# Keys and queries loaded as six adjacent tokens a partition instead of two, put in order by ScalarE's copies

## The chip, the cores and the metric

The kernel runs on one core of a Trainium2 chip. The metric is the device time of one execution in microseconds; lower is better. Engines are named as the profile names them: PE is TensorE's matmul, PEld its weight load, DVE is VectorE, ACT is ScalarE, POOL is GpSimd, SP is SyncE, whose queue issues most of the DMAs.

## What is computed

Four batches of attention with 8 heads, 768 tokens and 64 channels a head, followed by a Fourier mixing block with a two-layer network. All is fp32; the two weight matrices arrive as float64.

```
k_sum = max of k over blocks of 32 tokens      # 24 block keys a head
v_sum = mean of v over the same blocks
s_l   = q k^T / 8, only where |i - j| < 16
s_s   = q k_sum^T / 8 + log(32)
a     = softmax over [s_l, s_s];   attn = a [v, v_sum]
x     = attn as (batch, 768, 512)
u     = x + Re(FFT over tokens and channels of x)
un    = normalize(u) per token
out   = u + relu(un @ w_ch1) @ w_ch2           # 512 -> 2048 -> 512
```

## The kernel before

Heads are handled in pairs: batch b has pairs g = 0 to 3, and a pair's 2 x 64 channels fill the 128 partitions. For the scores, keys and queries must lie with channels on partitions and tokens along the row: `kt` (keys, with a margin of 16 zero columns at each end) and `qt` (queries). In HBM they lie the other way, token by token, so they are transposed on the chip.

**Loading.** `load(b, g)` fetches k, then q, of a pair into a tile `nat` of shape [128, 2, 3, 128] (four buffers; the profile calls its two uses `kn` and `qn`). Up to pair (2, 0), that is for 9 pairs and 18 DMAs of 384 KB, the layout is for TensorE: partition p of head e holds, for each of three groups j, the tokens 256j + 2p and 256j + 2p + 1. Two adjacent tokens are a run of 512 bytes in HBM. Later pairs are loaded in another layout and transposed by DVE; the change leaves them alone. Every load goes through `fetch` (L553) on SP's queue, for which the order of the program is kept in the first part of the kernel.

**Transposing.** `prepare(b, g)` makes kt and then qt.

- In batch 0 (`is_wide`), a matmul with the identity (L702) takes 64 channels of one head, one j and one parity s of the token, and writes 128 columns of a PSUM bank at every second place, so that the bank holds the tokens in order. Groups j = 0, 1 fill a bank of 512 columns, group 2 one of 256. A ScalarE copy (L704) brings each to SBUF, both sides consecutive.
- In batch 1 and pair (2, 0), a transpose (L710) turns both tokens at once, so that the parity s ends up in PSUM's partition half; two ScalarE copies (L712) of [64, 384] a head write to every second column of the destination: 8 copies a pair.

After that DVE takes the maximum over blocks of 32 keys (`km`, L717).

**Order.** `first_attention` lays out batch 0 by hand for PE and DVE: pair (0, 0)'s scores, the next pair's transposes, its scores, the values of the pair before, and so on. In `wide_scores` the scores are made in two halves of 384 tokens: matmuls of L733 (windows of 96 keys against 64 queries) and L737 (block keys), then an exponential on ACT (L739) and a product on DVE. `sum_values` brings block values to SBUF (L752, on ACT or DVE), and `wide_values` (L760) multiplies by the values `vw`, which are loaded in runs of 256 bytes. Then, in SP's order, come the Fourier tables `fs` and `fd` and the first weights (`words`), and the loads of batch 1's pairs.

Behind that, several generators run interleaved: the Fourier part of batch 0 (`y` L1193 with copies L1198, `mx` L1220, normalization L1264 on ACT and L1267 on DVE, transposes `unt` L1271), the conversion of float64 weights (L1052 to L1062 on DVE, L1054 and L1055 on ACT), the attention of batch 1 (scores L776, block scores L792, exponentials L782 and L793, values L809 and L814), and the network's first layer (`hx`, `hy`, `hz` L1293 with ACT copies L1304, L1309, L1311) and second (`o` L1335). Where a bank of L1293 is copied out by L1309 and then accumulated further, the later matmul waits for the copy.

Of the kernel before, what the change touches and what calls it, by code (L numbers as in the profile page):

```python
# [16 lines left out]
P = 128  # L17
# [473 lines left out]
def _main_program(ctx, tc, q, k, v, moe_w_ch1, moe_w_ch2, out):  # L491


    nc = tc.nc
    B, H, S, D = q.shape
    DM = H * D
    DF = moe_w_ch1.shape[1]
    NST = S // P
# [27 lines left out]
    ident = cpool.tile([P, P], FP, name="ident")  # L526
# [24 lines left out]
    def fetch(out, in_):  # L551

        ins = nc.sync.dma_start(out=out, in_=in_)  # L553
        if in_order[0]:
            tc.keep_in_program_order(ins)

    def abank(shape, name):
        return psum.tile(shape, FP, tag="attn", bufs=4, name=name)

    def bank(shape, name):  # L560
        return psum.tile(shape, FP, tag="bank", bufs=4, name=name)
# [12 lines left out]
    def load(b, g, *which):  # L574

        for n in which or (1, 0):
            t = nat[b, g, n] = apool.tile([P, 2, NST // 2, 2 * D], FP, tag="nat", bufs=4, name=f"{'qk'[n]}n_{b}_{g}")
            if (b, g) > (2, 0):
                t = nat[b, g, n] = t.rearrange("p e j n -> p (e j n)").rearrange("p (m c) -> p m c", c=32)
                for e in range(2):  # L580
                    for h in range(2):
                        r, o = D * e + 32 * h, (q, k)[n][b, 2 * g + e].offset + 32 * h
                        fetch(out=t[r:r + 32], in_=bass.AP((q, k)[n].tensor, o, [[D, 32], [32 * D, S // 32], [1, 32]]))
                continue
            fetch(out=t.rearrange("p e j n -> p (e j) n"),
                  in_=(q, k)[n][b, 2 * g:2 * g + 2].rearrange("e (j p s) d -> p (e j) (s d)", p=P, s=2))

# [95 lines left out]
    def prepare(b, g, *which):  # L685
        qn, kn = (nat[b, g, n] for n in range(2))
        kt, km = kt_bufs[g % 2], km_bufs[g % 2]
        qt = apool.tile([P, S], FP, tag="qt", name=f"qt_{b}_{g}") if 0 in (which or (0,)) else None
        for n in which or (1, 0):
            src, dst = (kn, kt[:, W:W + S]) if n else (qn, qt)  # L690
            if (b, g) > (2, 0):
                with tc.issue_after(marks["dense"]):
                    nc.vector.transpose(out=dst, in_=src.rearrange("p m c -> p (m c)"))
                continue
            if is_wide(b):
                for j0, j1 in ((0, 2), (2, 3)):
                    n = 2 * P * (j1 - j0)
                    ps = bank([P, n], f"qk_{b}_{g}_{j0}")
                    for j in range(j0, j1):
                        for s in range(2):  # L700
                            for e in range(2):
                                nc.tensor.matmul(ps[D * e:D * (e + 1), 2 * P * (j - j0) + s:2 * P * (j - j0 + 1):2],  # L702
                                                 src[:, e, j, D * s:D * (s + 1)], ident, start=True, stop=True)
                    nc.scalar.copy(out=dst[:, 2 * P * j0:2 * P * j1], in_=ps)  # L704
            else:
                for e in range(2):

                    ps = abank([P, S2], f"qk_{b}_{g}_{e}")
                    for j in range(NST // 2):
                        nc.tensor.transpose(ps[:, P * j:P * (j + 1)], src[:, e, j, :], ident)  # L710
                    for s in range(2):
                        nc.scalar.copy(out=dst[D * e:D * (e + 1), s:S:2], in_=ps[D * s:D * (s + 1)])  # L712
        if which == (0,):
            nat[b, g] = qt
            return
        with tc.issue_after(marks["fold", 0]) if (b, g) == (1, 0) else ExitStack():
            nc.vector.tensor_reduce(out=km[:, 0:nb], in_=kt[:, W:W + S].rearrange("p (n f) -> p n f", f=BLOCK),  # L717
                                    op=ALU.max, axis=AX.X)
        nat[b, g] = qt
# [110 lines left out]
    def first_attention():  # L830
# [3 lines left out]
        wt["fold"] = split_fold(0, fold)  # L834
        p = {0: wide_scores(0, 0, lambda: add_blocks(0))}
        prepare(0, 1)
        sum_values(0, 0)
        load(0, 3)
        for g in range(NP - 1):
            p[g + 1] = wide_scores(0, g + 1, (lambda: add_blocks(1)) if g == 1 else None)  # L840
            wide_values(0, g, p[g], x)
            load_values(*following(0, g, 2))
            for par in range(2):
                fold_sequence(par, g)
            if g == 0:
                get_tables(0)
            if g < NP - 2:
                prepare(0, g + 2)
                sum_values(0, g + 1)
            if g == NP - 3:  # L850
                load_raw(1)
                load(1, 0)
                load_raw(2)
                sum_values(0, g + 2)
# [105 lines left out]
    def gen_attention(b):  # L960
# [3 lines left out]
        if b == 2:  # L964
            load(2, 1)
            load(2, 2)
        for g in range(NP + 1):
# [36 lines left out]
            if n1:  # L1004
                prepare(*n1, *((1,) if b > 1 else ()))
# [388 lines left out]
    ps = bank([P, 512], "warm")  # L1394
# [19 lines left out]
    for vw in vw_bufs:  # L1414
        nc.gpsimd.tensor_copy(out=vw[:, :, D].rearrange("p (e n) -> p e n", e=2),
                              in_=count[:, None, :].to_broadcast([P, 2, NQ]))
# [47 lines left out]
    for b in range(B):  # L1464
# [14 lines left out]
        if b == B - 2:  # L1479
# [9 lines left out]
            ps = bank([1, 1], "flag_ps")  # L1489
# [42 lines left out]
```

## Time and profile before

| | us |
|---|---|
| median of 3 runs (807.29 to 811.65) | 810.48 |
| profiled execution | 811.17 |
| its span, first to last instruction | 809.3 |
| PE busy | 781.9 (97%) |
| PE weight loads busy | 571.9 (71%) |
| DVE busy | 500.8 (62%) |
| ACT busy | 224.3 (28%) |
| POOL busy | 46.8 (6%) |

Busy time is the union of an engine's instructions. The profile divides the span into 40 slices; the DMA engines are nine tenths busy or more in most of the first slices and less later. SP's hardware queue (q1) moved 133,920 packets and 118.53 MB. The 18 loads concerned are listed as `kn<-in_k_dram` x9 and `qn<-in_q_dram` x9, 384 KB each, with 5.4 and 7.8 us from issue to landing in the median. L712 appears with 40 copies of [64, 384], L704 with 8 of [128, 512] and 8 of [128, 256].

### The profile page before, as it was taken

What the parts mean: (1) busy time and instruction counts of PE and PEld (TensorE: products, weight loads), DVE (VectorE), ACT (ScalarE), POOL (GpSimd) and SP (SyncE); (2) the same over time, 40 slices, a digit from 0 to 9 for tenths busy, and PEclk for the clock granted to TensorE, in tenths of its full rate; (3) what the DMA queues carried; (4) which work ended last, traced back from release to release, by engine and by line L of the source; (5) the groups of instructions that cost most, each with busy time, mean ns of one, the idle gap of its engine ahead of it and who ended that gap; (6) DMA issues with size and microseconds to landing.
All of it is one profiled execution on the core that took longest, in us unless ns stands there. A gap on an engine that the chain in (4) does not pass through costs nothing.

```text
span 809.3 us, 14447 instructions
## 1 busy us (share of the span) xinstructions
PE 781.9 (97%) x5914; PEld 571.9 (71%) x5914; DVE 500.8 (62%) x1135; ACT 224.3 (28%) x493; POOL 46.8 (6%) x85
## 2 busy tenths in 40 slices
PE   8959899999999989999999999999999999999997
PEld 6758665555579856678669876688669875786686
DVE  5778998887998664554476734554476722532352
ACT  3523865543635112200126112200126102001200
POOL 0010000000000220010030300000030000000000
PEclk9979999999999999999999999999999999999999
DMA  9999799769655367939344248511514043205001
GB/s 218 222 198 179 162 320 271 155 224 298 214 165 174 93 202 184 206 86 173 117 176 153 66 160 174 156 48 53 227 40 153 37 171 149 87 0 228 0 28 55
DMA packets 135258, 121.83 MB, mean 151 GB/s; under 512 B 94448, under 2 KB 116688, under 8 KB 134992
## 3 DMA queue, kind: packets, MB, share of 16 engines
q1 hardware_dynamic: 133920, 118.53, 53.3%
q0 software_dynamic: 576, 2.10, 0.8%
q8 instruction: 48, 0.79, 0.4%
q10 hardware_dynamic: 688, 0.20, 0.1%
q14 instruction: 26, 0.21, 0.1%
HBM read 97.22 MB, written 23.59 MB: 149 GB/s over the span
## 4 chain that ended last, share of the span: by engine, by line
PE 89%; DVE 5%; ACT 2%; DMA 2%; SPq 1%; issue 1%; POOL 0%; DVEq 0%; ACTq 0%; POOLq 0%
PE hx L1293 20%; PE ox L1358 17%; PE hz L1293 10%; PE oz L1358 9%; PE o L1335 5%; PE hy L1293 5%; PE oy L1358 4%; PE y L1193 3%; PE sc L776 2%; PE mx L1152 2%; PE av L814 1%; PE av L809 1%; PE unt L1271 1%; DVE w L566 1%; SPq L553 1%; PE qk L702 1%
## 5 line engine op out<-in xcount | busy, mean ns | idle before, releaser
L1293 PE MATMUL hx<-u,w 128*128 128x384 f32 x512 | 187.2, 493 | 3.8 <-DVE h L566 3.8
L1293 PEld LDWEIGHTS hx<-u,w 128*128 128x128 f32 x512 | 95.7, 191 | 72.3 <-DVE h L566 5.7
L1293 PE MATMUL hz<-u,w 128*128 128x384 f32 x256 | 93.2, 487 | 0.0
L1358 PE MATMUL oz<-w,s 128*128 128x256 f32 x336 | 81.6, 380 | 0.6 <-DVE w L566 0.6
L1358 PE MATMUL ox<-w,s 128*128 128x256 f32 x336 | 80.3, 380 | 1.3 <-DVE x L566 1.3
L1358 PE MATMUL ox<-w,h 128*128 128x256 f32 x336 | 79.6, 380 | 0.0
L566 DVE TENSOR_TENSOR x<-ox,x 128x256 f32<-128x256 f32 x84 | 35.3, 422 | 69.5 <-PE ox L1358 69.2
L1293 PEld LDWEIGHTS hz<-u,w 128*128 128x128 f32 x256 | 48.5, 190 | 34.0 <-ACT h L1311 0.5
L1358 PEld LDWEIGHTS oz<-w,s 128*128 128x128 f32 x336 | 63.3, 190 | 10.6 <-issue 1.2
L1358 PEld LDWEIGHTS ox<-w,s 128*128 128x128 f32 x336 | 63.1, 190 | 10.7 <-DVE x L566 2.3
L1358 PEld LDWEIGHTS ox<-w,h 128*128 128x128 f32 x336 | 63.2, 190 | 9.6 <-DVE x L566 0.3
L1304 ACT COPY h<-hx 128x384 f32<-128x384 f32 x32 | 15.3, 479 | 169.9 <-PE hx L1293 169.9
L1293 PE MATMUL hy<-u,w 128*128 128x384 f32 x128 | 46.7, 488 | 0.0
L566 DVE TENSOR_TENSOR h<-hx,h 128x384 f32<-128x384 f32 x32 | 17.8, 555 | 46.4 <-PE hx L1293 46.1
L566 DVE TENSOR_TENSOR h<-hy,h 128x384 f32<-128x384 f32 x32 | 17.8, 555 | 45.3 <-PE hy L1293 45.3
L1320 ACT ACTIVATE h<-hx 128x384 f32<-128x384 f32 x32 | 15.7, 491 | 94.5 <-PE hx L1293 94.5
L1335 PE MATMUL o<-w,h 128*128 128x512 f32 x96 | 41.8, 593 | 0.0
L1358 PE MATMUL oy<-w,h 128*128 128x256 f32 x168 | 40.2, 379 | 0.0
L1293 PEld LDWEIGHTS hy<-u,w 128*128 128x128 f32 x128 | 24.1, 190 | 16.3
L566 DVE TENSOR_TENSOR x<-oz,x 128x256 f32<-128x256 f32 x42 | 17.7, 422 | 28.8 <-PE oz L1358 28.5
L1358 PEld LDWEIGHTS oy<-w,h 128*128 128x128 f32 x168 | 31.9, 190 | 4.3
L1335 PEld LDWEIGHTS o<-w,h 128*128 128x128 f32 x96 | 18.1, 190 | 21.9 <-issue 20.6
(164 smaller groups left out, 1099.5 us busy)
## 6 DMA issues: line engine op xcount, KB each, us to landing
w<-dw SPq DMA_DIRECT2D x44, 896.0 KB, 5.6
words<-in_moe_w_ch_dram SPq DMA_DIRECT2D x32, 512.0 KB, 6.6
dw<-w SPq DMA_DIRECT2D x12, 896.0 KB, 6.2
vw<-in_v_dram SPq DMA_DIRECT2D x47, 192.0 KB, 5.2
out_dram<-x SPq DMA_DIRECT2D x24, 256.0 KB, 2.2
vb<-in_v_dram SPq DMA_DIRECT2D x24, 192.0 KB, 4.0
kn<-in_k_dram SPq DMA_DIRECT2D x9, 384.0 KB, 5.4
qn<-in_q_dram SPq DMA_DIRECT2D x9, 384.0 KB, 7.8
```

The costliest lines, as they stand in the source:

```text
L553: ins = nc.sync.dma_start(out=out, in_=in_)
L566: return nc.vector.tensor_tensor(out=out, in0=in0, in1=in1, op=op).ins
L702: nc.tensor.matmul(ps[D * e:D * (e + 1), 2 * P * (j - j0) + s:2 * P * (j - j0 + 1):2], src[:, e, j, D * s:D * (s + 1)], ident, start=True, ...
L776: nc.tensor.matmul(ps[h][r:r + 64, i, :], kt[rows, o:o + 64], qt[rows, o:o + BLOCK], start=True, stop=True)
L809: nc.tensor.matmul(av[r][32 * j:32 * (j + 1), t, :], p[rows, h, i - NB2 * h, :], vw[rows, i, :], start=(t == 0), stop=False, skip_group_ch ...
L1152: nc.tensor.matmul(out, y[:, g], table, start=False, stop=True, skip_group_check=True)
L1193: nc.tensor.matmul(y, fgs[b][par][:, st, P * g:P * (g + 1)], fs[par][:, g % 2, st, :], start=(st == 0), stop=(st == n - 1))
L1293: ins = nc.tensor.matmul(ps, w[:, a, kk, :], u[:, r, kk, :], start=start and kk == 0, stop=stop and kk == 1, skip_group_check=True)
L1304: nc.scalar.copy(out=c11, in_=X)
L1320: nc.scalar.activation(out=c21, in_=X, func=AF.Relu)
L1335: nc.tensor.matmul(ps, h[:, n, hf, P * t:P * (t + 1)], wt[2, b, j][:, 2 * hf:2 * hf + 2, :], start=(n, hf) == (0, 0), stop=(n, hf) == (NC ...
L1358: nc.tensor.matmul(ps, left[a][:, n, :], wt[2, b, j][:, r, :], start=start and n == 0, stop=stop and n == NC - 1, skip_group_check=True)
```

## The change

Partition p now holds the six adjacent tokens 6p to 6p + 5 of a head, so that a run in HBM is 6 x 256 = 1536 bytes. The number of DMAs and their bytes stay. In batch 0 the matmuls write 128 consecutive columns for each of the six places c = 2j + s within a partition, and the copy puts them in order by writing with a step of six elements (24 bytes). In the later pairs the transposes stay as they are, and each copy's destination has a step of six elements within a group j, and of two between groups, where it had a step of two.

```diff
-            fetch(out=t.rearrange("p e j n -> p (e j) n"),
-                  in_=(q, k)[n][b, 2 * g:2 * g + 2].rearrange("e (j p s) d -> p (e j) (s d)", p=P, s=2))
+            fetch(out=t.rearrange("p e j n -> p e (j n)"),
+                  in_=(q, k)[n][b, 2 * g:2 * g + 2].rearrange("e (p j s) d -> p e (j s d)", p=P, s=2))
...
                             for e in range(2):
-                                nc.tensor.matmul(ps[D * e:D * (e + 1), 2 * P * (j - j0) + s:2 * P * (j - j0 + 1):2],
-                                                 src[:, e, j, D * s:D * (s + 1)], ident, start=True, stop=True)
-                    nc.scalar.copy(out=dst[:, 2 * P * j0:2 * P * j1], in_=ps)
+                                c = P * (2 * (j - j0) + s)
+                                nc.tensor.matmul(ps[D * e:D * (e + 1), c:c + P], src[:, e, j, D * s:D * (s + 1)], ident,
+                                                 start=True, stop=True)
+                    nc.scalar.copy(out=dst.rearrange("r (p c) -> r c p", c=NST)[:, 2 * j0:2 * j1],
+                                   in_=ps.rearrange("r (c p) -> r c p", p=P))
...
                     for s in range(2):
-                        nc.scalar.copy(out=dst[D * e:D * (e + 1), s:S:2], in_=ps[D * s:D * (s + 1)])
+                        nc.scalar.copy(out=dst[D * e:D * (e + 1)].rearrange("r (p j s) -> r s j p", j=NST // 2, s=2)[:, s],
+                                       in_=ps[D * s:D * (s + 1)].rearrange("r (j p) -> r j p", p=P))
```

## The prediction

> **What bounds the kernel now.** I began with busy time by stretch (columns: stretch and length in us, then busy us and instructions of PE, PEld, DVE, ACT, POOL, the granted TensorE clock, DMA share, GB/s).
>
> ```profile
> 5.00:41.00 36.00, 34.47 (x577) 27.21 (x576) 25.42 (x45) 16.75 (x34) 1.02 (x3) 1.00 1.03 228
> 41.00:55.00 14.00, 5.81 (x65) 4.95 (x62) 11.34 (x29) 3.38 (x7) 2.83 (x7) 0.74 0.97 190
> 55.00:170.00 115.00, 110.57 (x1084) 74.84 (x1084) 100.44 (x230) 67.37 (x136) 0.76 (x2) 0.97 0.87 228
> 170.00:810.00 640.00, 627.50 (x4191) 463.76 (x4189) 362.53 (x820) 135.57 (x316) 41.32 (x69) 0.99 0.45 131
> ```
>
> TensorE is busy nearly everywhere, so only its idle time can be won: 8.2 us of the 14 from 41 to 55, while the DMA share is 0.97. The changed loads and copies all lie before 170. PE's timeline shows what it waits for there (start, us, group, and in brackets the idle time with what ended it):
>
> ```profile
> 39.40 1.67 PE L760 MATMUL av<-vw,p 128*64 128x65 f32 x48
> 44.08 3.04 PE L760 MATMUL av<-vw,p 128*64 128x65 f32 x48 [3.01 <-DMA vw<-in_v_dram]
> 49.46 0.84 PE L710 MATMUL qk<-ident,kn 128*128 128x128 f32 x6 [2.34 <-DMA kn<-in_k_dram]
> 52.63 1.51 PE L710 MATMUL qk<-ident,qn 128*128 128x128 f32 x6 [2.32 <-DMA qn<-in_q_dram]
> ```
>
> Three transfers end three waits, 7.7 us together. From 5 to 41 no transfer holds PE; there it follows ScalarE closely. The ACT and PE timelines beside each other:
>
> ```profile
> 13.97 0.86 ACT L704 COPY kt<-qk 128x512 f32<-128x512 f32 x2 [0.17 <-PE qk L702]
> 15.29 0.86 ACT L704 COPY qt<-qk 128x512 f32<-128x512 f32 x2 [0.45 <-PE qk L702]
> 15.95 1.24 PE L733 MATMUL sc<-qt,kt 64*96 64x64 f32 x24
> ```
>
> The scores start at 15.95, after the first of qt's two copies and before the second has ended at 16.15. In the second batch the copies queue ahead of other ACT work:
>
> ```profile
> 79.73 2.06 ACT L712 COPY kt<-qk 64x384 f32<-64x384 f32 x4
> 81.82 2.07 ACT L712 COPY qt<-qk 64x384 f32<-64x384 f32 x4
> 83.92 0.81 ACT L1264 ACTIVATE big<-x,norm 128x512 f32<-128x512 f32 x1
> ...
> 84.78 2.27 PE L1271 MATMUL unt<-ident,big 128*128 128x128 f32 x11 [0.37 <-ACT big L1264]
> ```
>
> So ACT is busy only 28% of the span, yet a longer copy moves L1264, and PE is already waiting for it.
>
> [...] The new ScalarE copies write fp32 at a step of 24 bytes[...]; the old L712 writes at 8 bytes[...]. The trace [...] has no ScalarE write at a larger step of useful length. The nearest row is a VectorE read at 256 bytes, L634, against L717, which reads consecutively:
>
> ```profile
> L634 DVE TENSOR_REDUCE vbs<-vb x3: 1005/1010/1017, 81.3 to 130.8; 96x64 f32<-96x512 f32 x3
> ...
> L717 DVE TENSOR_REDUCE km<-kt x16: 933/944/950, 9.1 to 521.4; 128x24 f32<-128x768 f32 x16
> ```
>
> 1010/512 = 1.97 ns an element against 944/768 = 1.23: a factor of 1.6. [...] The trace disagrees for the old 8-byte step: 24 matmuls of L702 (two halves of the array side by side) take 23.39 - 22.08 = 1.31 us, 12 x 128 = 1536 columns a half, 0.85 ns each; consecutive hx takes 1.29 us for four of 384 columns, 0.84. [...]
>
> **The change part by part.**
>
> *Transfers.* Each of 18 loads (384 KB) goes from 768 runs of 512 bytes to 256 of 1536. From 28 to 29 us, with nearly only 512-byte packets, DMA moved 340 GB/s: 393/340 = 1.16 us a load. With 4632-byte runs (35 to 37 us) it moved 368, with 6144 (38 to 39) 385, so about 1.05 us now: 0.1 saved. Where queues are crowded (4 to 5 us, mostly such packets: 297 GB/s, 1.32 us) it may be 0.27. The lower bound is 0, since SP's queue is also held by issues of 256-byte vw loads, one of 6.14 us from 35.88. I take 0.16 a load: after the eight loads of batch 0 the vw load lands 1.3 us earlier, kn(1,0) 1.5 and qn(1,0) 1.7. Eight later loads have no wait of PE behind them: nothing. DMA issues stay the same in number; earlier vw issues find their buffers free (vw(0,2) at 27.16 needs av(0,0), done at 22.3).
>
> *PE.* L702 writes consecutively: no change, by the 0.85 and 0.84. L710 keeps its form.
>
> *Copies.* L704: 587 ns for 512 and 377 for 256 elements, so 0.82 ns an element. L712 takes 505 for 384. Bounds of the 24-byte step: nothing, or twice the per-element time (the 1.6 above is a whole instruction of a slower engine; its extra over 1.23, 0.74 ns, is near a second 0.82). [...] I take the double: +0.42, +0.21 and +0.32 us, 1.26 for a batch-0 pair and 2.5 for each of five later pairs, 17.6 us of ACT in all. Of this only what PE waits for counts.
>
> *Batch 0.* There is also a new wait: each L704 copy now fills every sixth token in turn, so the first half of the scores needs both copies of qt. Pair (0,0): kt 7.01 to 8.5, qt to 10.0, scores at 8.96 become 10.0: +1.05. (0,1): 13.97 + 3.0 = 17.0 for 15.95, +1.0. (0,2): 23.21 + 3.0 = 26.2 for 25.21, +1.0. (0,3): 34.7 for 33.93, of which 0.63 disappears in the wait for km at 36.06: +0.3. Sum 3.4; at unchanged copy speed 0.2 + 0.25 + 0.25 + 0 = 0.7. Behind the longer copies on ACT stand the value sums L752 and the exponentials; L752 is needed only an iteration later.
>
> *41 to 55.* av(0,3) starts at 41.07 + 3.4 = 44.5 with its vw landed (42.8), and without the idle time takes 1.67, not 3.04: done at 46.2 instead of 47.1. kn lands at 47.8, four kt copies run from 48.4 to 51.7, qn lands at 50.8, the first two qt copies end at 53.4, the scores follow, and y (L1193), at 55.01 before, starts at 53.9: **-1.1**. DVE's fold for y's first half ended at 51.9 and moves 0.9 earlier, so it isn't late next. The 3.4 lost thus vanish in waits for transfers.
>
> *77 to 170.* Pair (1,1): eight copies ahead of L1264, +2.5, straight onto PE (unt at 84.78). (1,2): kt and qt from 94.40 delay the copy L1309 from 99.13 to 101.7; hx at 100.08 accumulates in the bank which it reads, and starts at 102.2: +2.1, which contains the 0.6 of the transposes at 95.49. (1,3): transposes at 114.45 behind two kt copies +0.6; scores at 128.70, which already wait 1.02 for qt, behind six: +1.9. (2,0): copies from 161.5 lie beside L1335, nothing (2.5 if that cover went). Sum **+7.1**. PE has only 1.9 us of idle time between 90 and 170 that could absorb any; I deduct none.
>
> Sum -1.1 + 7.1 = **+6.0 us**. The profiled execution took 811.17 (span 809.3, 1.9 around it), so 817.2; the median 810.48 lies 0.7 lower, so **816.5**.
>
> **The rivals.**
> *Copies at unchanged rate.* [...] Then batch 0 loses 0.7, av(0,3) runs at 42.8, kn and qn land at 47.8 and 50.8, qt is ready at about 52.8 and y starts 1.7 earlier: 808.8. With 0.27 a load, 2.7 earlier: 807.8. This is the one that isn't slower. It decides by one number: from -1.7 to +6.0 with the extra share f of a full doubling, zero at f = 1.7/7.7 = 0.22, a 64x384 copy of 0.58 us.
> *A part of the penalty* (a third): -1.7 + 2.6 = +0.9, 811.4. [...]
> *Runs are longer but transfers aren't earlier*, since vw packets and issues set the stream: the -1.1 goes and some 0.6 is added, 818.2 with slow copies. For it: DMA moves only 51 GB/s from 42 to 44 us.
> *Knock-on:* late conversions L1054 and L1055 feed DVE, busy 100.44 of 115 us; with the cover of (2,0) gone too, +5 more, 821.5.
>
> **How the numbers follow.** Doubled copies 0.70 (with or without earlier transfers, knock-on included), a part 0.08, unchanged rate 0.22. About 0.5% (4.05 us) is what a measurement can tell from no change. Doubled: 0.8 of it above that, the rest within. Part: half above, half within. Unchanged: 0.3 faster, 0.65 within, 0.05 slower. Slower 0.56 + 0.04 + 0.01 = 0.61; faster 0.07; within 0.32. The range 807 to 822 reaches from just past the best of the unchanged rate to the knock-on. The doubled copies' own range is 812.5 to 822.
>
> **What would show it.** In the profile after: L712 near 820 ns and L704 near 1010 and 590 (505, 587 and 377 would make the forecast wrong); about 18 x 512 = 9,200 fewer packets on q1 than 133,920; PE's wait before av(0,3) gone; y starting 1 to 2 us before 55.0; unt behind L1264 some 2.5 us later against y. A y later than 55 would say that the transfers gained nothing.

## The result and the profile after

The changed kernel is **slower**: 824.21 us (median of 6 runs, 819.11 to 824.62) against 809.63 us for the kernel before on the same chip (6 runs, 807.29 to 812.57), a ratio of 1.0159 [1.0125, 1.0192], or +14.6 us. The forecast was +6.0, and 824 lies above its range. The profiled execution took 821.57 us (span 819.7), 10.4 us more than the profiled one of before; the steps below are followed through these two executions. In the kernel after, a line number is 1 to 3 higher: L702 is now L703, L704 is L705, L710 is L712, L712 is L714, L760 is L763, L1193 is L1196, L1264 is L1267, L1309 is L1312.

Two rows of the page of the kernel after:

```profile
PE 785.9 (96%) x5914; PEld 573.1 (70%) x5914; DVE 501.0 (61%) x1135; ACT 242.1 (30%) x493; POOL 46.6 (6%) x85
...
PEclk8989799999999999999999999999999999999999
```

ACT has 17.8 us more than its 224.3; the forecast said 17.6. But PE is busy 4.0 us longer than its 781.9 **for the same 5914 instructions**, and its granted clock has 8s where before had `9979` and then only 9s. That was in no sum of the prediction. Busy time by stretch, in the columns of the prediction (stretch, length, busy time and count of PE, PEld, DVE, ACT, POOL, then granted clock, DMA share, GB/s):

```profile
5.00:41.00 36.00, 30.90 (x473) 24.11 (x472) 20.43 (x39) 18.53 (x29) 1.02 (x3) 0.91 0.97 230
41.00:55.00 14.00, 9.75 (x167) 7.36 (x167) 12.50 (x27) 8.77 (x13) 1.25 (x5) 0.92 0.91 222
55.00:170.00 115.00, 104.34 (x1049) 72.10 (x1050) 95.68 (x222) 67.86 (x122) 2.26 (x3) 0.92 0.70 193
```

From 5 to 41 the clock is 0.91 for 1.00. From 41 to 55 PE idles 4.3 us for 8.2; but the windows stand at fixed times, and part of what fills this one is work of batch 0 that before was done by 41 (473 matmuls from 5 to 41, for 577). From 55 to 170 it idles 10.7 us where it had 4.4, with a clock of 0.92 for 0.97. The groups of kt's copies, and SP's queue in the list of queues (group, count | busy us, mean ns of one | idle time before them and what ended it; the queue: packets, MB, share):

```profile
L714 ACT COPY kt<-qk 64x384 f32<-64x384 f32 x20 | 17.1, 853 | 3.9 <-PE qk L712 3.5
L705 ACT COPY kt<-qk 128x512 f32<-128x512 f32 x4 | 4.4, 1111 | 5.8 <-PE qk L703 5.8
L705 ACT COPY kt<-qk 128x256 f32<-128x256 f32 x4 | 2.8, 690 | 0.0
...
q1 hardware_dynamic: 124704, 118.53, 51.4%
```

The copies took 853, 1111 and 690 ns for 505, 587 and 377: about 1.7 ns an element for 0.82, the doubling that the forecast took. The queue moved 9,216 packets fewer. A single copy of batch 0 took more than the 1010 and 590 forecast, but a pair of them overlaps: the two keep ACT busy for 1.56 us where it was 0.86, +0.70 for the 0.63 forecast. The loads and the copies are thus about what the prediction said; the error lies in what became of them.

PE's timeline of the kernel after, at the end of batch 0 (start, us, group, in brackets the idle time and what ended it):

```profile
11.59 1.24 PE L740 MATMUL sc<-qt,km 64*32 64x384 f32 x4 [1.14 <-DVE km L720]
...
45.76 3.07 PE L763 MATMUL av<-vw,p 128*64 128x65 f32 x96
48.76 0.88 PE L712 MATMUL qk<-ident,kn 128*128 128x128 f32 x6
51.74 0.52 PE L712 MATMUL qk<-ident,qn 128*128 128x128 f32 x3 [2.10 <-issue]
...
54.90 2.94 PE L1196 MATMUL y<-fs,fold 128*128 128x193 f32 x8
```

The last values of batch 0 and the kn transposes no longer wait for a transfer: both brackets of before, 3.01 and 2.34, are gone. Still y starts at 54.90, hardly earlier than 55.01. Further on, ACT's and PE's timelines beside each other:

```profile
80.55 3.45 ACT L714 COPY kt<-qk 64x384 f32<-64x384 f32 x4
84.03 3.41 ACT L714 COPY qt<-qk 64x384 f32<-64x384 f32 x4
87.47 0.81 ACT L1267 ACTIVATE big<-x,norm 128x512 f32<-128x512 f32 x1
...
85.78 1.03 PE L812 MATMUL av<-vw,p 64*32 64x65 f32 x48 [1.30 <-ACT qt L714]
88.33 2.61 PE L1274 MATMUL unt<-ident,big 128*128 128x128 f32 x11 [1.12 <-ACT big L1267]
...
106.88 1.56 PE L1296 MATMUL hx<-u,w 128*128 128x384 f32 x4 [0.89 <-ACT h L1312]
...
134.96 1.19 PE L812 MATMUL av<-vw,p 64*32 64x65 f32 x94 [0.99 <-ACT qt L714]
137.87 1.46 PE L779 MATMUL sc<-qt,kt 64*64 64x32 f32 x26 [1.72 <-ACT qt L714]
```

PE waits where the forecast looked: for L1267, for L1312, for qt. It also waits at L812 until a copy of qt is done, though the values read neither kt nor qt: in the program they share the four PSUM banks of `abank` with the transposes, so they need a bank which the copies have not yet emptied (1.30 us at 85.78, 0.99 at 134.96). Set against the same instructions of before, the delay grows like this:

| PE instruction | before | after | later by |
|---|---|---|---|
| first eight of y | 55.01 | 54.90 | -0.11 |
| y's group of 28 | 58.80 | 59.56 | +0.76 |
| unt, 11, behind (1,1)'s copies | 84.78 | 88.33 | +3.55 |
| unt, the next 12 | 89.07 | 93.37 | +4.30 |
| hx behind the copy of its bank, (1,2) | 100.08 | 106.88 | +6.80 |
| kn transposes of (1,3) | 114.45 | 121.64 | +7.19 |
| scores, 26, behind (1,3)'s copies | 128.70 | 137.87 | +9.17 |
| first o (L1335, L1338 after) | 148.91 | 159.68 | +10.77 |
| end of the span | 809.3 | 819.7 | +10.4 |

Everything is lost before 160. Four steps of the table have a wait for a slow copy ahead of them: 2.73 from y's last matmuls (65.68, and 66.50 after: +0.82) to unt, then 2.50, 0.39 and 1.98, **7.6 together**, for 7.1 forecast (some tenths of it are a lower clock inside these steps). Three others have none, and PE runs without a bracket there: +0.87 in y, +0.75 in unt, +1.60 behind the scores. The windows on these stretches, in the columns above, first after and then around the same instructions before:

```profile
54.90:59.56 4.66, 4.66 (x15) 4.66 (x15) 4.66 (x13) 1.89 (x4) 2.16 (x3) 0.50 1.08 352
88.00:96.00 8.00, 7.67 (x149) 6.76 (x149) 5.06 (x15) 4.79 (x9) 0.00 (x0) 0.64 0.52 103
137.80:144.00 6.20, 6.13 (x56) 4.14 (x57) 3.65 (x7) 1.93 (x5) 0.00 (x0) 0.72 0.81 291
```

```profile
55.01:58.80 3.79, 3.79 (x16) 3.79 (x15) 2.50 (x7) 1.18 (x4) 0.75 (x2) 0.62 0.83 181
84.00:92.00 8.00, 7.55 (x178) 6.56 (x178) 7.11 (x22) 5.73 (x10) 0.00 (x0) 0.79 1.00 209
128.70:135.00 6.30, 6.30 (x61) 4.07 (x62) 5.89 (x12) 3.39 (x7) 0.00 (x0) 1.00 0.95 365
```

The granted clocks are 0.50, 0.64 and 0.72, where before they were 0.62, 0.79 and 1.00.

### The profile page after: what moved, and what is told of

It is laid out like the page before. It is cut to its first block, busy times and chain, and to the rows that moved or that the text cites. A ratio compares the mean times of both kernels' runs of the same rounds, so it can differ in the third digit from the quotient of the medians.

```text
span 819.7 us, 14447 instructions
## 1 busy us (share of the span) xinstructions
PE 785.9 (96%) x5914; PEld 573.1 (70%) x5914; DVE 501.0 (61%) x1135; ACT 242.1 (30%) x493; POOL 46.6 (6%) x85
## 4 chain that ended last, share of the span: by engine, by line
PE 89%; ACT 4%; DVE 4%; DMA 2%; issue 1%; ACTq 0%; DVEq 0%
PE hx L1296 20%; PE ox L1361 17%; PE hz L1296 10%; PE oz L1361 9%; PE o L1338 5%; PE hy L1296 5%; PE oy L1361 4%; PE y L1196 3%; PE sc L779 3%; PE mx L1155 2%; PE av L812 2%; PE av L817 1%; PE unt L1274 1%; ACT qt L714 1%; PE sc L736 1%; ACT kt L714 1%
## 5 line engine op out<-in xcount | busy, mean ns | idle before, releaser
L1361 PEld LDWEIGHTS ox<-w,s 128*128 128x128 f32 x336 | 63.1, 190 | 10.7 <-DVE x L566 2.3
L566 DVE TENSOR_TENSOR h<-hx,h 128x384 f32<-128x384 f32 x32 | 17.8, 556 | 46.3 <-PE hx L1296 46.1
L566 DVE TENSOR_TENSOR h<-hy,h 128x384 f32<-128x384 f32 x32 | 17.8, 556 | 45.3 <-PE hy L1296 45.3
L1338 PE MATMUL o<-w,h 128*128 128x512 f32 x96 | 41.8, 593 | 0.0
L566 DVE TENSOR_TENSOR x<-oz,x 128x256 f32<-128x256 f32 x42 | 17.8, 423 | 28.8 <-PE oz L1361 28.5
L785 ACT ACTIVATE p<-sc 128x384 f32<-128x384 f32 x24 | 10.7, 488 | 79.3 <-PE sc L779 79.3
```

Source lines behind the costliest of these rows:

```text
L566: return nc.vector.tensor_tensor(out=out, in0=in0, in1=in1, op=op).ins
L785: nc.scalar.activation(out=p[:, h], in_=ps[h], func=AF.Exp, scale=SC)
L1338: nc.tensor.matmul(ps, h[:, n, hf, P * t:P * (t + 1)], wt[2, b, j][:, 2 * hf:2 * hf + 2, :], start=(n, hf) == (0, 0), stop=(n, hf) == (NC ...
L1361: nc.tensor.matmul(ps, left[a][:, n, :], wt[2, b, j][:, r, :], start=start and n == 0, stop=stop and n == NC - 1, skip_group_check=True)
```

## The experiments

All were timed beside the kernel before on the same chip, and each ratio is to that. Three explanations stood at first: the copies' 24-byte step costs it all, waits plus what follows from them (theory A in the expectations); or the loads cost too (theory B); or any large step does, on the PSUM side as well.

**One half of the change each.** `e1_loads_only` has the two new fetch lines and the old matmuls and copies; `e2_copies_only` has all but the fetch lines. Both leave the tokens in a permuted order; the number of instructions stays. `half_of` in the expectations is a small table that DVE waits for before it makes the first km.

> Loads as in the changed kernel (six adjacent tokens a partition), transposes and copies as before, so that keys and queries come out in a permuted order of tokens (that part of the computation is changed). Theory A, the copies at a 24-byte step and what hangs on them are the whole loss: copies 587, 377 and 505 ns as before, the time 0 to 2.7 us below before (transfers land some 1.5 to 3 us earlier in the wait from 41 to 55 us). Theory B, the new transfers also cost, by moving small transfers such as half_of behind them: slower than before by 2 us or more.

> Transposes and copies as in the changed kernel, loads in the old runs of 512 bytes, so that the order of tokens is permuted. Theory A: copies 853 ns, the time above before by as much as the changed kernel (14.6 us) or 1 to 3 us more, since the earlier landings are missing. Theory B: below the changed kernel, some 6 to 10 us above before, with half_of landing near 9.0 us as before.

e1 took 808.67 us, ratio 0.9977 [0.9961, 0.9994], with copies of 587, 376 and 507 ns. e2 took 824.03, ratio 1.0171 [1.0136, 1.0206], with copies of 1115, 700 and 856. So the whole loss comes with the copies and matmuls, and the 1536-byte runs by themselves bring about 0.2%.

**The same order of tokens, written in memory order.** `e3_walk` keeps the kernel after and turns the copies' loops: SBUF is now written in runs of four or two neighbouring elements every 24 bytes (L705) or at a step of 8 bytes (L714), and PSUM is read at a step of 512 bytes.

```diff
-  out=dst.rearrange("r (p c) -> r c p", c=NST)[:, 2 * j0:2 * j1], in_=ps.rearrange("r (c p) -> r c p", p=P)
+  out=dst.rearrange("r (p c) -> r p c", c=NST)[:, :, 2 * j0:2 * j1], in_=ps.rearrange("r (c p) -> r p c", p=P)
...
-  .rearrange("r (p j s) -> r s j p", j=NST // 2, s=2)[:, s], in_=ps[...].rearrange("r (j p) -> r j p", p=P)
+  .rearrange("r (p j s) -> r s p j", j=NST // 2, s=2)[:, s], in_=ps[...].rearrange("r (j p) -> r p j", p=P)
```

> The changed kernel with one edit: each copy walks its destination in the order of memory (runs of neighbouring or every second element) and reads PSUM at a step of 512 bytes instead of writing SBUF at 24. Theory A with the write step as the cause: copies back at 505, 587 and 377 ns, the time 0 to 3 us below before. If any large step costs, on the PSUM side too: copies near 850 ns and the time 10 to 15 us above before. Theory B: faster than the changed kernel, still 2 us or more above before.

e3 took 807.99 us, ratio 0.9971 [0.9954, 0.9988]: **faster than both kernels**, with the same loads, the same matmuls and the same elements copied. Its groups:

```profile
L714 ACT COPY kt<-qk 64x384 f32<-64x384 f32 x20 | 10.1, 505 | 8.7 <-PE qk L712 8.3
L705 ACT COPY kt<-qk 128x512 f32<-128x512 f32 x4 | 2.5, 626 | 5.4 <-PE qk L703 5.4
L705 ACT COPY kt<-qk 128x256 f32<-128x256 f32 x4 | 1.6, 404 | 0.0
```

505, 626 and 404 ns: this order, with its PSUM read at 512 bytes, costs nothing to 7% more than the copies of before, so it was the SBUF write at 24 bytes that cost the doubling. The same kernel's timeline shows what the loads bring when the copies don't eat it:

```profile
42.11 1.79 PE L763 MATMUL av<-vw,p 128*64 128x65 f32 x48 [0.71 <-DMA vw<-in_v_dram]
47.20 1.51 PE L712 MATMUL qk<-ident,kn 128*128 128x128 f32 x6 [3.29 <-DMA kn<-in_k_dram]
...
52.02 2.94 PE L1196 MATMUL y<-fs,fold 128*128 128x193 f32 x8
```

y starts 3.0 us earlier than before in this execution; over its 22 runs the kernel keeps 0.29%, 2.3 us.

**The order made by TensorE instead.** `e4_pe_order` leaves batch 0 as before; in the later pairs the loads are new, the transposes write PSUM at every third column (12 bytes), and the copies are the old ones.

```diff
-  nc.tensor.transpose(ps[:, P * j:P * (j + 1)], src[:, e, j, :], ident)
+  nc.tensor.transpose(ps[:, j:S2:NST // 2], src[:, e, j, :], ident)
```

> Batch 0 wholly as before; pairs (1,0) to (2,0) loaded as six adjacent tokens, put in order by TensorE: the transposes write PSUM at a step of three elements (12 bytes), the copies are those of before. If a PSUM write at 12 bytes is free: L710 at 272 ns, copies 505 ns, the time within 1.5 us of before. If it slows the transposes: L710 near 400 to 550 ns, some 2 to 6 us above before. Both theories: no late half_of here.

It took 811.72 us, ratio 1.0015 [0.9991, 1.0039]. The mean of a transpose was 309 and 306 ns for kn and qn (279 and 306 before, and 309 and 306 in e3, which writes consecutively); the copies took 507 and 509. The 12-byte write thus has no cost that can be told from the scatter of the clock; nor is there a gain, with only 10 of the 18 loads changed.

**Where the slow copies cost.** A further explanation (theory C in the expectations) was that the lateness of batch 0 is carried to the end. `e5_slow_first` is e3 with the 24-byte copies in batch 0 only, `e6_slow_later` with them in (1,0) to (2,0) only: each keeps one of e3's two edits.

> New loads; the copies of batch 0 write at 24 bytes as in the changed kernel, those of pairs (1,0) to (2,0) walk memory in order as in e3. Theory A, batch 0's lateness vanishes in the waits for transfers before y: L705 near 1117 and 680 ns, L714 near 505, PE some 3 us later at the last values of batch 0, y within 1 us of its start in e3, the time 807 to 811. Theory C, lateness of batch 0 is carried to the end (with the stretches at half clock that it starts): 4 to 7 us above before.

> New loads; the copies of batch 0 walk memory in order, those of pairs (1,0) to (2,0) write at 24 bytes. Theory A: L714 853 ns, the waits at unt, at the transposes of (1,2), at hx after L1312 and at the scores of (1,3) as in the changed kernel, some 7.5 us, and stretches at half clock behind them, 3 to 6 us more by PE's busy time: 820 to 824, nearly the whole loss. If the clock is no cause of its own: 7.5 - 2 = 5.5 us above before, some 816. Theory C: 814 to 817.

e5 took 807.07 us, 0.9965 [0.9942, 0.9987], as e3; e6 took 820.89, 1.0144 [1.0116, 1.0172], which is 1.73% above e3 by the two ratios (e3 ran on another chip). The 24-byte copies of batch 0 cost nothing that can be measured. In e5's timeline the lateness is there, and gone again:

```profile
44.48 1.78 PE L763 MATMUL av<-vw,p 128*64 128x65 f32 x48 [1.41 <-DMA vw<-in_v_dram]
...
52.80 2.94 PE L1196 MATMUL y<-fs,fold 128*128 128x193 f32 x8
```

The values start 2.4 us later than in e3, y 0.8 later. In between PE waits less for the kn transfer, 2.48 us for 3.29, and no longer for qn, 0.94 in e3.

The later pairs cost nearly all of it. e3 and e6 differ in the order within L714's copies alone, so their timelines can be read side by side, from (1,3)'s scores on, first e3 and then e6:

```profile
126.25 1.00 PE L779 MATMUL sc<-qt,kt 64*64 64x32 f32 x26 [1.02 <-ACT qt L714]
127.17 1.56 PE L1296 MATMUL hx<-u,w 128*128 128x384 f32 x4
...
130.87 0.81 PE L1296 MATMUL hx<-u,w 128*128 128x384 f32 x2
```

```profile
135.29 1.70 PE L779 MATMUL sc<-qt,kt 64*64 64x32 f32 x26 [1.72 <-ACT qt L714]
136.92 2.93 PE L1296 MATMUL hx<-u,w 128*128 128x384 f32 x4
...
143.91 1.49 PE L1296 MATMUL hx<-u,w 128*128 128x384 f32 x2
```

From the first to the last of these lines e3 takes 4.62 us and e6 8.62. No line in between has a wait: the same four hx matmuls occupy 2.93 us for 1.56. The windows on the two stretches (the columns above) give the reason:

```profile
126.20:131.00 4.80, 4.75 (x57) 3.34 (x58) 4.80 (x10) 1.92 (x4) 0.00 (x0) 1.00 0.98 396
```

```profile
135.20:144.00 8.80, 8.71 (x57) 5.68 (x58) 3.67 (x7) 1.96 (x5) 0.00 (x0) 0.50 0.51 193
```

57 matmuls each, at a granted clock of 1.00 in e3 and **0.50** in e6. Ahead of it PE idled 0.99 and 1.72 us within 3 us in e6 (at 132.39 and 135.29), and 1.02 in e3. Over the whole span PE is busy 786.1 us in e6 and 780.6 in e3, 5.5 of the 14.0 us between their spans (820.1 and 806.1).

**The later pairs one by one.** The same mix with the slow copies in (1,3) only (e7), in (1,0) and (2,0) (e8), in (1,1) and (1,2) (e9), by a condition on (b, g) in L714's patterns:

```diff
+  to = "j p" if (b, g) == (1, 3) else "p j"     # e8: in ((1, 0), (2, 0)); e9: in ((1, 1), (1, 2))
```

> As e3, with the 24-byte copies in pair (1,3) alone. Waits that these copies add to PE, read in e6 against before: 0.4 at the transposes, 1.3 at the values (L812), 0.7 at the scores (L779), 2.4 us together. Theory A with the clock: behind them PE runs at half clock for some 7 to 10 us, its busy time grows by 3 to 5 us over e3, and the time is 5 to 7.5 us above e3, about 813 to 815.5. Without the clock as a cause: 2.4 us above e3, about 810.5, and PE's busy time that of e3.

> As e3, with the 24-byte copies in pairs (1,0) and (2,0) alone. Theory A: (2,0) lies beside L1338 and costs nothing; (1,0) stands before y and costs the 1 to 1.5 us by which y started later in e6 than in e3. Time 0 to 2 us above e3.

> As e3, with the 24-byte copies in pairs (1,1) and (1,2) alone. Theory A with the clock: waits of 1.6 + 0.4 at L812, 0.9 at unt, 1.2 at the transposes and 1.1 at hx, 5.2 us, and half clock from about 84 us on, 1 to 3 us: 6 to 8 us above e3, 814 to 816. Without the clock: 5 us, and PE's busy time that of e3.

| slow copies in | us | ratio to before | above e3 | waits forecast |
|---|---|---|---|---|
| (1,3) | 813.12 | 1.0029 [1.0011, 1.0047] | 0.58%, 4.7 us | 2.5 |
| (1,0), (2,0) | 810.15 | 1.0003 [0.9983, 1.0023] | 0.32%, 2.6 us | 0 |
| (1,1), (1,2) | 813.68 | 1.0050 [1.0031, 1.0070] | 0.79%, 6.4 us | 4.6 |
| sum | | | 1.69%, 13.7 us | 7.1 |
| all five (e6) | 820.89 | 1.0144 [1.0116, 1.0172] | 1.73%, 14.0 us | |

The parts add up to the whole. Each costs some 2 us more than its waits, but a single difference to e3, put together from two intervals, is itself uncertain by some 2 us; e6's excess over the waits, 6.9 us with 2.7 either way, is clear. For (1,3) the expectation was 2.4 us without the clock and 5 or more with it; 4.7 came. Its profile shows 2.7 us of waits and then 3.0 us more lost behind the scores, where PE is never idle. The windows there, e7 first and then e3:

```profile
132.00:139.00 7.00, 7.00 (x32) 3.97 (x31) 2.08 (x5) 2.75 (x6) 0.00 (x0) 0.51 0.39 138
```

```profile
128.00:135.00 7.00, 7.00 (x57) 4.10 (x56) 6.59 (x12) 3.91 (x8) 0.00 (x0) 1.00 0.67 257
```

In e7's 22 runs the same instructions spread from 809.87 us at a mean clock of 0.991 to 816.99 at 0.981: the seven runs at 0.989 or more have a median of 810.27, the eight at 0.985 or less 815.03. e9 landed at 6.4 where 5 (waits alone) and 6 to 8 (with the clock) had been set against each other. Its one profiled execution took 811.29 us, 2.4 less than its median, and has no extra busy time (780.9). The other runs have no trace, but a mean clock: the six runs at 0.989 or more have a median of 811.7 us, the seven at 0.983 or less 816.6. (1,0) and (2,0) came out a little above the 0 to 2 expected, within the uncertainty; the span of e8's profiled execution is only 0.6 us above e3's.

**How much is the clock.** The kernel before spreads with its clock too (of its 48 runs beside e7 to e9, 25 at 0.989 or more have a median of 808.5 us, 13 at 0.985 or less 812.95), so a spread by itself doesn't speak against the slow copies. What goes with them is a lower middle: the median clock is 0.989 in e3 and in those runs of before, 0.9865 in e7, 0.986 in e9, 0.9805 in e6 and 0.9785 in the kernel after. A straight line through e7's 22 runs falls by 0.58 us for each 0.001 of clock, as does one through the 48. By that slope, as an estimate, the clock is 4.9 of e6's 14.0 us and 6.1 of the change's 14.6. What is left, 9.1 and 8.5, is somewhat more than the waits.

## Why the prediction was wrong in size

**Right: the copies.** A doubling per element was taken from two bounds and came, 17.8 us of ACT for 17.6, with 853 ns for 505. That it would double, and the weight of 0.70 on it, were the author's estimate: no row of before has a ScalarE write at such a step, and L634, the nearest, is a read by another engine. The rival of the unchanged rate (808.8) is refuted by the same rows. On the PSUM side the 8 bytes of L702 had shown no cost (0.85 ns a column for 0.84), and neither did 12 bytes in e4 (309 and 306 ns a transpose, as in e3).

**Right: the waits from 77 to 170**, 7.6 us for 7.1, though one kind was missed. At (1,1) and (1,3) part of the time is lost at L812, behind banks that the copies hold, and not at unt or at the scores. The forecast followed only the instructions that read the copies' results. The bank was a second way for the same lateness, so the sum hardly changed; that it didn't was luck, since the bank was in no term of it.

**Right in the main: batch 0's lateness vanishes in waits for transfers** (e5 equals e3). That the order of tokens makes the first scores wait for both qt copies did no harm for the same reason.

**Wrong: -1.1 at y**; -0.1 was measured. In this execution the first km came late (the 1.14 us at L740 above; DVE had waited 8.3 us for `half_of`, 6.9 before), and PE ran from 11 to 19 at a clock of 0.57; batch 0 ended some 6 us late instead of 3.4. With that the waits for transfers were used up, and another path held y: the step says that DVE's fold moves 0.9 us earlier and isn't late next, but the fold of the last values began at 52.96 for 49.06, 3.9 later, and the chain that ended last runs from those values through DVE to y without a transfer. That is not a rule: with the new loads, y starts between 51.0 and 55.7 in the single profiled executions of e1, e3 and e5 to e9, and in e1, with no slow copy, at 55.7. The step gave one number where executions scatter by 4.7 us. e5 and e6, which have each half of the slow copies, start y 0.8 and 1.4 us later than e3, so that an estimate for both, 52.02 + 2.2 = 54.2, is near the 53.9 forecast; with such a scatter that may be chance.

**Wrong: the step "Sum -1.1 + 7.1 = +6.0".** This is the step that failed most. It priced each new wait at its idle time alone and took all PE work behind it at its duration of before. The missing term is the granted clock. In the profiled execution it is 0.87 + 0.75 + 1.60 = 3.2 us: with 7.6 of waits, -0.1 at y and -0.4 after 160 that makes the 10.4 (the rounded terms give 10.3). Of it the 0.87 in y need not come from the slow copies, since e3 has it too (4.67 us from y to its group of 28, 4.66 in the kernel after, 3.79 before); 2.35 us have no such counterpart. Between the medians it is larger, about 6 by the estimate above. Their difference, 14.6, is 4.2 more than 10.4, since the profiled run of before (clock 0.987) lies 1.5 us above its median and that of after (0.980) 2.6 below: it was the second fastest of the six, four of which lie at 824.1 to 824.6 us with clocks of 0.978 and 0.979. The prediction did use this effect once, in its favour: av(0,3) at 1.67 us instead of 3.04 once the idle time ahead of it goes (the kernel after, with no idle time there, was granted 1.00 from 45.76 to 48.80, where before had 0.53 from 44.0 to 47.2). It was not applied to the waits that it added.

**What stays open.** The stretches at about half clock behind (1,3)'s scores in e6, e7 and the kernel after (0.50 and 0.51 in the windows above, 0.57 from 139.2 to 142.0) begin at new idle time or up to 2 us behind it, and e3, with the same instructions in the same order, has none there. No run created an idle time by other means or filled one up, so that the idle time triggers the fall is argued from where the stretches lie, not shown by itself. The kernel before has a stretch at 0.60 too, from 84.78 to 89.07, behind a wait of 1.80 us at 82.42. Nor do the runs tell how much idle time it takes: 1.02 us in one place was not followed by it (e3), 0.99 and 1.72 within 3 us was (e6). What makes the granted clock fall, and what lets it rise again, no run here shows.

## What to carry to other kernels

Where ScalarE puts elements in order, try it with SBUF written in memory order and the large step on the PSUM side: here the same permutation of 384 elements then took 505 (e3) instead of 853 ns (the kernel after). Price a new wait of TensorE by its idle time, and reckon with a lower clock for the work behind it: in e6 8.8 us at 0.50 came behind waits of 0.99 and 1.72 us, in e3 1.00 was granted behind one of 1.02. The whole loss of e6 was about twice the waits (14.0 us for 7.1). Lateness ahead of a transfer that PE waits for anyway cost nothing measurable (e5, 0.9965 for the 0.9971 of e3). An engine that is 28% busy could still move the end, by 14.6 us: follow what its longer instruction delays, the readers of its result and the next user of the bank that it reads.

## What was not expected of the hardware

- ScalarE's copy of 384 elements that reads PSUM at a step of 512 bytes took 505 ns (e3), as the one of before, which reads consecutively; a consecutive read with the write to SBUF at 24 bytes took 853 (the kernel after).
- A transpose's write to PSUM at 12 bytes took no longer than a consecutive one, within the scatter (means of 309 and 306 ns for kn and qn in e4, the same in e3, 279 and 306 before).
- Two idle times of 1 to 2 us within 3 us were followed by 8.8 us at a granted clock of 0.50 (e6), in a kernel that keeps PE 96% busy.
- Three times longer runs in HBM for 18 of the loads, 9,216 packets fewer, were worth 0.2 to 0.3% (e1, e3).
